# Order of PSUM banks and copies where the lag shrinks, and a new order of the last chunk, in a fused attention and mixture-of-adapters kernel

## The chip, the core and the metric

The kernel runs on one core of a Trainium2 chip. The metric is device time in microseconds for one launch, taken as the median of several runs. Each engine (PE for matrix products, DVE for vector work, ACT for activations, POOL, and SP, which issues most transfers) works through its own list of instructions in order and waits on semaphores of the others.

## What is computed

Attention over pooled keys, followed by a mixture of eight low-rank adapters with the two best kept per token:

```python
kv_pool = kv.reshape(B, H // r, r, W // r, r, C).mean(axis=(2, 4))
kv_flat = kv_pool.reshape(B, -1, C) @ w_sr            # keys and values
a = softmax(q @ k.T / sqrt(C));  x = a @ v
logits = x @ w_gate                                   # the 2 best of 8 experts
out = x + sum over the 2 experts of w_e * (x @ A[e]) @ B[e]
```

There are 4 batches of 12288 tokens with 128 features; each batch has 768 pooled keys. The result is 49152 x 128 in float32.

## The kernel before, in words

The tokens go in 96 chunks of 512 (`NCH` = 96), 24 to a batch. A software pipeline runs over the loop variable `c`. In each pass PE makes the scores of a later chunk (line 329, three pairs of products, each followed by an exponential on ACT, line 330), weighs the values of chunk c-1 in two halves (`weigh`, line 341), and turns x of chunk c-2 (`turned`, line 408: four products with the identity into the bank `tp`). After the second half of `weigh`, DVE normalises chunk c-1: a reciprocal (line 348), the multiplication into `xn_all` (line 352), and four MAX8 (line 359). The sums of `weigh` have one pair of banks (`ps_x`, one buffer), so the first product of the next pass waits until line 352 has read them.

The adapter part of chunk x is done later, by a lag that shrinks with x because the gates travel through DRAM and back:

- `gated_hidden(x)` (lines 440 to 449): one product of A with the turned x (line 443), and one DVE operation that multiplies by the gates and writes `ht` (line 446). It is done in pass x + lag(x).
- `up(x)` (line 489): four products of `ht` with B; then `give(x)`: DVE adds x (line 503) into `osb`, and every second time SP stores a pair of chunks (line 522).
- `evacuate` (line 419): DVE copies the turned x out of its bank into `xt`, of which there are seven buffers.

Both `gated_hidden` and `up` use the one bank of `mtile` (tag `hd`) unless they are given another; the turned x uses the one bank of `ps_t` (tag `tp`, also got by `t_bank()`). The lag is 9 for x below 57, 8 below 67, 7 below 81, then 6 (line 675). Where it falls by one, a pass gets two of something. From lines 677 to 679: passes 65, 74 and 87 have two `gated_hidden`, and passes 69, 78 and 91 have two `up`. In these six passes a second piece of work goes into the bank `tp` (line 708), which the turned x of the same pass needs a little later. In every pass the order of the DVE list is: adds of `up`, normalise, last `gated_hidden`, (in odd passes) the transpose of the gates, then the copy of line 419.

The last two chunks, n-1 = 94 and n = 95, are done behind the loop in an order written out by hand (lines 834 to 911), with banks of their own. There every chunk is stored by itself, 256 KB each: the chunks n-7 to n-1 by SP in the order n-7, n-5, n-6, n-3, n-2, n-1, n-4, and chunk n by ACT's queue (line 911). `take` (line 494) copies a finished bank to `osb` on ACT, `turn` (line 795) turns h by products with the identity and copies it out on ACT (line 801) or DVE (line 803), `x_first` (line 481) puts x into a bank by products with the identity so that B's product is added on top. `all_ok` (lines 578 to 584) counts range flags with two products and two small DVE operations, whose result `bad` every engine loads (line 915) to decide on a slow path that isn't taken here. The two DVE operations of `count_sum(1)` (lines 571 and 572) belong to the same check.

Of the kernel before, what the change touches and what calls it, by code (L numbers as in the profile page):

```python
# [21 lines left out]
def kernel(  # L22
# [11 lines left out]
    P = 128  # L34
    B, N, C = q.tensor.shape
# [5 lines left out]
    NTOK = 512  # L41
    NS = NTOK // P
# [3 lines left out]
    NCH = B * CPB  # L46
# [16 lines left out]
        name="ps_x", bufs=1, side="right", space=bass.MemoryType.PSUM))  # L63
# [5 lines left out]
    def mtile(shape, dtype=FP32, name="hd"):  # L69
        return ps_h.tile(shape, dtype, tag="hd", name=name)  # L70

    mm = nc.tensor.matmul
# [75 lines left out]
    id_f32 = const.tile([P, P], FP32)  # L148
# [111 lines left out]
    def squares(b, t):  # L260

        v = vext[b][:, 2 * t:2 * t + 2, 0:C + G]
        sq = keep.tile([P, 2, C + G], FP32, name=f"sq{b}") if t == 0 else small.tile(
            [P, 2, C + G], FP32, tag="sq", name="sq", bufs=1)
        nc.gpsimd.tensor_tensor(sq, v, v, op=ALU.mult)
        if t == 0:
            sqsum[b] = sq
        else:
            nc.gpsimd.tensor_tensor(sqsum[b], sqsum[b], sq, op=ALU.add)
# [45 lines left out]
    tt, xps, xpair, xn, gw, gin, xT, hg, hgT, hps = {}, {}, {}, {}, {}, {}, {}, {}, {}, {}  # L315
# [124 lines left out]
    def gated_hidden(c, bank=None):  # L440

        h_ps = mtile([P, NS, P], name="h_ps") if bank is None else as_tokens(bank)
        mm(h_ps, a_bf, xT[c], start=True, stop=True)  # L443
        hgT[c] = run.tile([P, NS, P], BF16, tag="ht", name="ht", bufs=4)
        h = c % 2 * NS // 2
        nc.vector.scalar_tensor_tensor(  # L446
            hgT[c].rearrange("p (k a) t -> p k (a t)", k=2),
            gE[c // 2][:, h:h + NS // 2].rearrange("p a t k -> p k (a t)"), 1.0,
            h_ps.rearrange("p (k a) t -> p k (a t)", k=2), op0=ALU.add, op1=ALU.mult)

    def as_tokens(bank):
        return bank.rearrange("p (s c) -> p s c", s=NS)
# [22 lines left out]
    dps = {}  # L475

    def x_first(c, bank, lo, hi):

        dps[c] = as_tokens(bank) if lo == 0 else dps[c]
        for s in range(lo, hi):  # L480
            mm(dps[c][:, s], id_f32, xn[c][:, s, 0:C], start=(s == 0), stop=False,
               skip_group_check=True)

    def up(c, bank=None):
        fresh = c not in dps
        if fresh:
            dps[c] = mtile([P, NS, P], name="d_ps") if bank is None else as_tokens(bank)
        for s in range(NS):
            mm(dps[c][:, s], columns(hgT[c], c, s), b_bf, start=(s == 0 and fresh),  # L489
               stop=(s == NS - 1), skip_group_check=True)  # L490

    def take(c, lo=0, hi=NS):
        osb = half_out()
        nc.scalar.activation(osb[:, lo:hi], dps[c][:, lo:hi], AF.Copy)
        return osb
# [10 lines left out]
    def put(c, osb, lo=0, hi=NS, queue=None):  # L506
        t0 = c // 2 * HROWS
        (queue or nc.sync).dma_start(
            out[t0:t0 + HROWS, :].rearrange("(p k s) c -> p k s c", p=P, k=2)[:, c % 2, lo:hi],
            osb[:, lo:hi])  # L510
# [28 lines left out]
    CUT = NCH - 15  # L539
# [38 lines left out]
    def all_ok(bank):  # L578
        n = (NCH - CUT) * NS
        mm(bank[0:1, 0:n], ones_c, ok[:, tail], start=True, stop=False)  # L580
        mm(bank[0:1, 0:n], ones_c, low, start=False, stop=True)
        nc.vector.tensor_reduce(last, bank[0:1, 0:n], axis=AX.X, op=ALU.add)
        full = float(P * (NCH * NS + n) + P * 2 * B + 2 * B)
        nc.vector.tensor_scalar(bad, last, tot, full, op0=ALU.add, op1=ALU.not_equal)
# [17 lines left out]
    def t_bank():  # L602
        return ps_t.tile([P, NTOK], FP32, tag="tp", name="t_ps")
# [72 lines left out]
    sent, fetched, made, ups = {}, {}, {}, {}  # L676
# [9 lines left out]
    for c in range(2, NCH - 1):  # L686
        b, k = divmod(c, CPB)
        if c in fetched and lag(2 * fetched[c] + 1) > 8:
            load_gates(fetched[c])
        if c % 2 == 0 and c // 2 + 3 < 2 * NQ:  # L690
            turn_q(c // 2 + 3)
        if c % 2 and (c + 11) // 2 < 2 * NQ:
            load_q((c + 11) // 2)
        if c == 2:
            load_q(6)
        next_scores()
        weigh(c - 1, 0)
        if c == NCH - 2:
            down(c - 4, stile("h_ps")[:, 0])
            apply_gate(c - 4)  # L700
        next_scores()
        if c in tanhs:
            gate_tanhs(tanhs[c])
        two = len(made.get(c, ())) > 1
        if two:
            gated_hidden(made[c][0])
        for x in ups.get(c, ()):
            up(x, t_bank() if two or x != ups[c][0] else None)
            give(x)
        if c in fetched and lag(2 * fetched[c] + 1) <= 8:  # L710
            load_gates(fetched[c])
        weigh(c - 1, 1)
        prep_step(c)
        if c == CUT + 5:
            count_sum(0)
        normalise(c - 1)
        if c % 2 == 0:
            gate(c // 2 - 1, nc.gpsimd)
            if c // 2 + 4 < 2 * NQ:
                cast_q(c // 2 + 4)  # L720
        _, evacuate = turned("x", c - 2)
        if c == NCH - 2:
            _, evacuate_h = turned("h", c - 4, stile("t_ps")[:, 0])
        next_scores()
        prep(c)
        k0 = 19
        if k in (k0, k0 + 2, k0 + 4) and b + 1 < B:
            if b == 0:
                squares(0, (k - k0) // 2)
            squares(b + 1, (k - k0) // 2)  # L730
        for x in made.get(c, ())[-1:]:
            gated_hidden(x)
        if c in sent:
            send_gates(sent[c])
        if c == NCH - 2:
            down(c - 3, stile("h_ps")[:, 0])
            apply_gate(c - 3)
        evacuate(c == NCH - 2)
        if c == NCH - 2:
            evacuate_h(True)  # L740

        if c in (32, 40, 56, 80):
            ranges((32, 40, 56, 80).index(c))
        a = slice(0, CUT * NS)
        if CUT < c <= CUT + 3:
            count_ok(a, c - CUT - 1, flags[:, 0:1])
        elif c == CUT + 4:
            values_ok()
        elif c == CUT + 5:
            count_sum(1)  # L750


# [4 lines left out]
        name="ps_e", bufs=1, reuse_waits="tile", space=bass.MemoryType.PSUM))  # L757

    def bank(i):
        return ps_e.tile([P, NTOK], FP32, tag=f"e{i}", name=f"e{i}")  # L760
# [30 lines left out]
    def turn(src, lo, hi, bank_, store, key, act=True):  # L791

        t_ps = bank_.bitcast(BF16)[:, 0:(hi - lo) * P].rearrange("p (s c) -> p s c", c=P)
        for s in range(lo, hi):
            mm(t_ps[:, s - lo], src[:, s], id_bf, is_transpose=True,
               start=(s == lo), stop=(s == hi - 1), skip_group_check=True)
        if key not in store:
            x_or_h = ("xt", 7) if store is xT else ("ht", 4)
            store[key] = run.tile([P, NS, P], BF16, tag=x_or_h[0], name="xr", bufs=x_or_h[1])
        if act:  # L800
            nc.scalar.activation(store[key][:, lo:hi], t_ps, AF.Copy)
        else:
            nc.vector.tensor_copy(store[key][:, lo:hi], t_ps)
# [10 lines left out]
    n = NCH - 1  # L814
# [8 lines left out]
    def tops4(c, top, y):  # L823
# [20 lines left out]
        name="ps_f", bufs=1, side="right", space=bass.MemoryType.PSUM))  # L844

    def fbank(i):
        return ps_f.tile([P, NTOK], FP32, tag=f"f{i}", name=f"f{i}")

    _, evacuate = turned("x", n - 2)
# [36 lines left out]
    x3 = ps_e.tile([P, 2, 512], FP32, tag="y5", name="x3")  # L886
# [2 lines left out]
    gate_w(0, NS, nc.gpsimd, arg5, msk5)  # L889
    gated(n, 0, NS, arg5, h5)  # L890
    x_first(n - 1, fbank(1), 2, 4)
    up(n - 1)
    o4 = take(n - 1)
    put(n - 1, o4)
    add(n - 4, o1, nc.gpsimd)
    put(n - 4, o1)
    d5 = as_tokens(x3[:, 1])
    for s in range(2):
        mm(d5[:, s], id_f32, xn[n][:, s, 0:C], start=(s == 0), stop=False, skip_group_check=True)
    turn(hg[n], 0, 2, bank(0), hgT, n)  # L900
    turn(hg[n], 2, 4, t_bank(), hgT, n, False)
    all_ok(bank(1))
    for s in range(2):
        mm(d5[:, s], hgT[n][:, s], b_bf, start=False, stop=(s == 1), skip_group_check=True)
    o5 = half_out()
    nc.scalar.activation(o5[:, 0:2], d5[:, 0:2], AF.Copy)
    d6 = as_tokens(mtile([P, NTOK], name="d6"))
    for s in range(2, 4):
        mm(d6[:, s - 2], hgT[n][:, s], b_bf, start=(s == 2), stop=(s == 3), skip_group_check=True)
    nc.vector.tensor_tensor(o5[:, 2:4], d6[:, 0:2], xn[n][:, 2:4, 0:C], op=ALU.add)  # L910
    put(n, o5, queue=nc.scalar)

    end_banks.close()
    ps_g = ctx.enter_context(tc.tile_pool(name="ps_g", bufs=1, space=bass.MemoryType.PSUM))
# [3 lines left out]
    with tc.If(bad_v != 0):  # L918
# [11 lines left out]
        with tc.For_i(0, B) as b:  # L930
            nc.sync.dma_start(kp, kp_all[bass.ds(b, 1)].rearrange("o p k -> p (o k)"))
            for h in range(2):
                s = slice(h * NKV // 2, (h + 1) * NKV // 2)
# [3 lines left out]
            for h in range(2):  # L937
                v_ps = mtile([P, NJ // 2, C + E], name="gv_ps")
                for g in range(NJ // 2):
                    j = h * NJ // 2 + g  # L940
                    mm(v_ps[:, g], kp[:, j * P:(j + 1) * P], wext,
                       start=(g == 0), stop=(g == NJ // 2 - 1))
# [96 lines left out]
```

## Time and profile before

| what | value |
|---|---|
| median of 3 runs | 373.58 us (373.55 to 374.5) |
| the profiled execution | 374.4 us, span 372.6 us from first to last instruction |
| mean granted clock of PE | 0.999 |
| busy: PE, ACT, DVE, POOL | 355.7, 308.3, 300.3, 223.7 us |
| idle before line 330 (ACT), until PE gave the scores | 37.7 us |
| idle before line 503 (DVE), until PE gave the products of `up` | 31.9 us |
| moved by DMA | 101.01 MB, mean 271 GB/s |

Busy times are sums over the span; PE's matrix products are pipelined and their ends are modelled, so the start of the next product tells more than an end. Times given as "250.24" are microseconds from the start of the span. Rows of a timeline read: start, length, engine, line, operation, out<-in, and in brackets the engine's idle time before it and what ended it. The span is 1.8 us shorter than the execution's own time.

### The profile page before, as it was taken

What the parts mean: (1) busy time and instruction counts of PE and PEld (TensorE: products, weight loads), DVE (VectorE), ACT (ScalarE), POOL (GpSimd) and SP (SyncE); (2) the same over time, 40 slices, a digit from 0 to 9 for tenths busy, and PEclk for the clock granted to TensorE, in tenths of its full rate; (3) what the DMA queues carried; (4) which work ended last, traced back from release to release, by engine and by line L of the source; (5) the groups of instructions that cost most, each with busy time, mean ns of one, the idle gap of its engine ahead of it and who ended that gap; (6) DMA issues with size and microseconds to landing.
All of it is one profiled execution on the core that took longest, in us unless ns stands there. A gap on an engine that the chain in (4) does not pass through costs nothing.

```text
span 372.6 us, 10601 instructions
## 1 busy us (share of the span) xinstructions
PE 355.7 (95%) x3945; PEld 264.3 (71%) x3945; DVE 300.3 (81%) x953; ACT 308.3 (83%) x390; POOL 223.7 (60%) x374
## 2 busy tenths in 40 slices
PE   4889999999999999999999999999999999999984
PEld 1456777777777777777777777777777767767773
DVE  3785558878888888888888888888788889988894
ACT  1579999889888888889889889898887978978843
POOL 1013799978599879693497879693454235223253
PEclk9999999999999999999999999999999999999999
DMA  7998999999999999999999999998678699754324
GB/s 264 419 354 218 318 289 311 302 298 276 288 375 294 316 305 303 285 298 294 305 316 305 349 341 285 319 274 266 207 213 277 195 244 231 215 132 130 144 114 173
DMA packets 83818, 101.01 MB, mean 271 GB/s; under 512 B 58804, under 2 KB 59060, under 8 KB 83764
## 3 DMA queue, kind: packets, MB, share of 16 engines
q1 hardware_dynamic: 83332, 99.98, 93.6%
q8 instruction: 31, 0.51, 0.6%
q10 hardware_dynamic: 432, 0.33, 0.3%
q14 instruction: 23, 0.19, 0.1%
HBM read 62.33 MB, written 25.90 MB: 237 GB/s over the span
## 4 chain that ended last, share of the span: by engine, by line
PE 87%; DVE 5%; ACT 3%; DMA 2%; issue 1%; POOL 1%; SPq 0%; ACTq 0%; DVEq 0%
PE xps L341 34%; PE sg L329 32%; PE t_ps L408 6%; PE h_ps L443 5%; PE d_ps L489 5%; DMA kvt<-in_kv_dram 2%; ACT tt L330 2%; DVE osb L503 1%; PE v_ps L218 1%; DVE ht L446 1%; DVE kvt L194 1%; PE k_ps L243 1%; PE w_ps L609 1%; PE kp_ps L210 0%; ACT qT L597 0%
## 5 line engine op out<-in xcount | busy, mean ns | idle before, releaser
L330 ACT ACTIVATE tt<-sg 128x1024 f16<-128x1024 f32 x288 | 276.3, 1023 | 38.0 <-PE sg L329 37.7
L329 PE MATMUL sg<-qT,kfT 128*128 128x512 f16 x576 | 170.2, 379 | 0.5 <-ACT qT L597 0.3
L341 PEld LDWEIGHTS <-tt 128*128 128x128 f16 x2304 | 146.6, 98 | 26.9 <-DVE xn_all L352 15.4
L341 PE MATMUL xps<-vext,tt 128*128 128x136 f16 x2256 | 164.6, 223 | 0.3 <-DVE xn_all L352 0.2
L503 DVE TENSOR_TENSOR osb<-d_ps,xn_all 128x512 f32<-128x512 f32 x82 | 56.7, 691 | 32.0 <-PE d_ps L489 31.9
L368 POOL TENSOR_TENSOR arg<-xn_all,top 128x64 f32<-128x64 f32 x47 | 14.4, 307 | 99.9 <-DVE top L359 93.4
L352 DVE TENSOR_TENSOR xn_all<-xps,rinv_all 128x540 f32<-128x540 f32 x94 | 67.7, 720 | 3.3
L329 PEld LDWEIGHTS <-kfT 128*128 128x128 f16 x576 | 49.1, 98 | 24.6 <-issue 1.8
L194 POOL TENSOR_TENSOR kvt<-kvt 128x1024 f32<-128x1024 f32 x27 | 63.7, 2361 | 2.0 <-PE xps L341 1.9
L446 DVE SCALAR_TENSOR_TENSOR ht<-ge,h_ps 128x512 bf16<-128x512 f16 x90 | 60.5, 672 | 1.3 <-PE h_ps L443 0.9
L108 POOL CAST q<-q 128x1024 f16<-128x1024 f32 x45 | 46.8, 1041 | 24.1 <-DMA q<-in_q_dram 24.1
L489 PEld LDWEIGHTS <-ht 128*128 128x128 bf16 x368 | 27.7, 98 | 21.3 <-issue 1.3
L359 DVE MAX8 top<-xn_all 128x8 f32<-128x8 f32 x376 | 35.1, 156 | 6.3
L408 PE MATMUL t_ps<-id_bf,xn_all 128*128 128x128 bf16 x376 | 36.3, 219 | 2.5 <-DVE osb L503 2.5
L419 DVE COPY xt<-t_ps 128x512 bf16<-128x512 bf16 x92 | 36.8, 400 | 0.0
L443 PE MATMUL h_ps<-xt,a_bf 128*128 128x512 bf16 x90 | 34.1, 379 | 0.1
L489 PE MATMUL d_ps<-b_bf,ht 128*128 128x128 bf16 x328 | 31.7, 219 | 0.0
L408 PEld LDWEIGHTS <-xn_all 128*128 128x128 bf16 x376 | 26.1, 98 | 3.6 <-issue 3.3
L348 DVE RECIPROCAL rinv_all<-xps 128x4 f32<-128x4 f32 x94 | 17.1, 182 | 12.9 <-PE xps L341 11.5
L371 POOL TENSOR_SCALAR msk<-msk 128x64 f32<-128x64 f32 x47 | 20.1, 428 | 4.1
L372 POOL TENSOR_TENSOR arg<-arg,msk 128x64 f32<-128x64 f32 x47 | 15.0, 320 | 3.9
L370 POOL TENSOR_TENSOR arg<-arg,msk 128x64 f32<-128x64 f32 x47 | 15.0, 319 | 3.7
(150 smaller groups left out, 221.0 us busy)
## 6 DMA issues: line engine op xcount, KB each, us to landing
kvt<-in_kv_dram SPq DMA_DIRECT2D x48, 512.0 KB
q<-in_q_dram SPq DMA_DIRECT2D x46, 512.0 KB
out_dram<-osb SPq DMA_DIRECT2D x44, 512.0 KB
ge<-g_h SPq DMA_DIRECT2D x45, 256.0 KB
out_dram<-osb SPq DMA_DIRECT2D x7, 256.0 KB
q<-in_q_dram SPq DMA_DIRECT2D x1, 1024.0 KB
qT<-q SPq DMA_TRANSPOSE x46
g_h<-g_sb SPq DMA_DIRECT2D x45, 16.0 KB
```

Of the source, the lines that this page charges most:

```text
L108: nc.gpsimd.tensor_copy(q16[i], q32[i].rearrange("p k n -> p (k n)"))
L194: eng.tensor_tensor(v[:, 0], v[:, 0], v[:, d], op=ALU.add)
L329: mm(sg[:, k], kfT[b][:, j * P:(j + 1) * P], qc, start=True, stop=True)
L330: nc.scalar.activation(tt[c][:, 2 * r:2 * r + 2], sg, AF.Exp, bias=0.0, scale=scale)
L341: mm(o, tt[c][:, j, s * P:(s + 1) * P], vext[b][:, j, 0:VW], start=(j == 0 and s % 2 == 0), stop=(j == NJ - 1 and s % 2 == 1), skip_group_ ...
L352: nc.vector.tensor_tensor(xn[c][:, :, 0:C + G].rearrange("p (b s) v -> p b s v", b=2), xv[:, :, :, 0:C + G], ri.rearrange("p (b s) -> p b ...
L408: mm(columns(t_ps, c, s), src[:, s], id_bf, is_transpose=True, start=(s == 0), stop=(s == NS - 1), skip_group_check=True)
L419: nc.vector.tensor_copy(to, t_ps)
L443: mm(h_ps, a_bf, xT[c], start=True, stop=True)
L446: nc.vector.scalar_tensor_tensor(hgT[c].rearrange("p (k a) t -> p k (a t)", k=2), gE[c // 2][:, h:h + NS // 2].rearrange("p a t k -> p k ( ...
L489: mm(dps[c][:, s], columns(hgT[c], c, s), b_bf, start=(s == 0 and fresh), stop=(s == NS - 1), skip_group_check=True)
L503: nc.vector.tensor_tensor(osb[:, lo:hi], d, xn[c][:, lo:hi, 0:C], op=ALU.add)
```

## The change

There are two parts. In the six passes, the extra piece of work in bank `tp` is now the first of the pass and the last piece takes `hd`: in passes 65, 74 and 87 the first `gated_hidden` goes to `tp` and `up` to `hd`; in passes 69, 78 and 91 the first `up` goes to `tp` and the second to `hd`. In the pass ahead of each (64, 68, 73, 77, 86, 90) the copy of line 419 is put on DVE's list before the last `gated_hidden` instead of behind it. `count_sum(1)` moves from pass 86 to pass 88.

In the tail, the products that put the first half of x of chunk n into its bank now come ahead of `up(n-1)` (and in another bank); the products that turn the last h come directly behind `up(n-1)`; `take(n-1)` and the stores of n-1 and n-4 follow behind the turn, so on ACT the copy of the turned h stands ahead of `take(n-1)`. The two DVE operations of the range check stand behind the last store.

```diff
+    def flag(bank):
+        n = (NCH - CUT) * NS
         nc.vector.tensor_reduce(last, bank[0:1, 0:n], axis=AX.X, op=ALU.add)
...
-        two = len(made.get(c, ())) > 1
-        if two:
-            gated_hidden(made[c][0])
+        for x in made.get(c, ())[:-1]:
+            gated_hidden(x, t_bank())
         for x in ups.get(c, ()):
-            up(x, t_bank() if two or x != ups[c][0] else None)
+            up(x, None if x == ups[c][-1] else t_bank())
             give(x)
...
+        early = max(len(made.get(c + 1, ())), len(ups.get(c + 1, ()))) > 1
+        if early:
+            evacuate()
         for x in made.get(c, ())[-1:]:
             gated_hidden(x)
...
-        evacuate(c == NCH - 2)
+        if not early:
+            evacuate(c == NCH - 2)
...
-        elif c == CUT + 5:
+        elif c == CUT + 7:
             count_sum(1)
...
     x_first(n - 1, fbank(1), 2, 4)
+    d5 = bank(0)
+    x_first(n, d5, 0, 2)
     up(n - 1)
+    turn(hg[n], 0, 2, x3[:, 1], hgT, n)
+    turn(hg[n], 2, 4, t_bank(), hgT, n, False)
     o4 = take(n - 1)
     put(n - 1, o4)
     add(n - 4, o1, nc.gpsimd)
     put(n - 4, o1)
-    d5 = as_tokens(x3[:, 1])
-    for s in range(2):
-        mm(d5[:, s], id_f32, xn[n][:, s, 0:C], start=(s == 0), stop=False, skip_group_check=True)
-    turn(hg[n], 0, 2, bank(0), hgT, n)
-    turn(hg[n], 2, 4, t_bank(), hgT, n, False)
-    all_ok(bank(1))
+    count = mtile([P, NTOK], name="count")
+    all_ok(count)
+    d5 = dps[n]
     for s in range(2):
         mm(d5[:, s], hgT[n][:, s], b_bf, start=False, stop=(s == 1), skip_group_check=True)
...
-    d6 = as_tokens(mtile([P, NTOK], name="d6"))
+    d6 = as_tokens(bank(1))
...
     put(n, o5, queue=nc.scalar)
+    flag(count)
```

## The prediction, made before the changed kernel ran

> **What bounds the kernel now.** I read the page first, then the waits of PE, then the timeline around the passes that the change touches, then the end.
>
> ```profile
> span 372.6 us, 10601 instructions
> PE 87%; DVE 5%; ACT 3%; DMA 2%; issue 1%; POOL 1%; SPq 0%; ACTq 0%; DVEq 0%
> ```
>
> The chain that ended last runs through PE for 87% of the span. In the loop a gap on PE is therefore lost time, unless another engine would have stopped PE a little later anyway. PE's list of waits has one entry that fits the change:
>
> ```profile
> PE t_ps L408 <- DVE osb L503: 2.5, 6, 0.4
> ```
>
> Six times the turning of x (line 408) waits until DVE's add (line 503) has read the bank `tp`. These are the six passes with a second piece of work in that bank. Pass 64, an ordinary one, and pass 65 stand side by side in the timeline:
>
> ```profile
> 246.65 0.87 PE L341 MATMUL xps<-vext,tt 128*128 128x136 f16 x12
> 247.36 0.39 PE L408 MATMUL t_ps<-id_bf,xn_all 128*128 128x128 bf16 x4
> 247.78 0.72 DVE L352 TENSOR_TENSOR xn_all<-xps,rinv_all 128x540 f32<-128x540 f32 x1
> 248.02 0.38 PE L443 MATMUL h_ps<-xt,a_bf 128*128 128x512 bf16 x1
> 248.53 0.37 DVE L359 MAX8 top<-xn_all 128x8 f32<-128x8 f32 x4
> 248.66 0.87 PE L341 MATMUL xps<-vext,tt 128*128 128x136 f16 x12
> 248.82 0.67 DVE L446 SCALAR_TENSOR_TENSOR ht<-ge,h_ps 128x512 bf16<-128x512 f16 x1
> 249.41 0.42 DVE L419 COPY xt<-t_ps 128x512 bf16<-128x512 bf16 x1
> 249.81 0.38 PE L443 MATMUL h_ps<-xt,a_bf 128*128 128x512 bf16 x1
> 250.02 0.39 PE L489 MATMUL t_ps<-b_bf,ht 128*128 128x128 bf16 x4
> 250.22 0.69 DVE L446 SCALAR_TENSOR_TENSOR ht<-ge,h_ps 128x512 bf16<-128x512 f16 x1 [0.39 <-PE h_ps L443]
> 250.24 0.87 PE L341 MATMUL xps<-vext,tt 128*128 128x136 f16 x12
> 250.83 0.68 DVE L503 TENSOR_TENSOR osb<-t_ps,xn_all 128x512 f32<-128x512 f32 x1
> 251.43 0.17 DVE L348 RECIPROCAL rinv_all<-xps 128x4 f32<-128x4 f32 x1
> 251.56 0.38 PE L408 MATMUL t_ps<-id_bf,xn_all 128*128 128x128 bf16 x4 [0.45 <-DVE osb L503]
> 251.63 0.72 DVE L352 TENSOR_TENSOR xn_all<-xps,rinv_all 128x540 f32<-128x540 f32 x1
> 252.86 0.34 PE L341 MATMUL xps<-vext,tt 128*128 128x136 f16 x3
> ```
>
> In pass 64 the turn starts 247.36 - 246.65 = 0.71 after `weigh`'s second half; in pass 65 it starts 251.56 - 250.24 = 1.32 after. So 0.61 is lost, more than the row's 0.45, as that counts from a modelled end. From the turn to the next pass's first L341 both passes take 1.30.
>
> A pass with two `up` has the same pattern (pass 78):
>
> ```profile
> 297.40 0.87 PE L341 MATMUL xps<-vext,tt 128*128 128x136 f16 x12
> 298.71 0.38 PE L408 MATMUL t_ps<-id_bf,xn_all 128*128 128x128 bf16 x4 [0.44 <-DVE osb L503]
> 298.78 0.72 DVE L352 TENSOR_TENSOR xn_all<-xps,rinv_all 128x540 f32<-128x540 f32 x1
> 300.01 0.87 PE L341 MATMUL xps<-vext,tt 128*128 128x136 f16 x12
> ```
>
> **The six passes, step by step.** No instruction is added or removed; two change places.
>
> *The stall goes.* In pass 65 bank `tp` is now filled by the first product (249.81) and emptied by the first DVE operation instead of the second. That one ends at 250.22 + 0.69 = 250.91. DVE's end at 251.51 let PE start at 251.56, so a release costs 0.05: the bank is free at 250.96. The turn would come by itself at 250.24 + 0.71 = 250.95. In pass 78 it is the first add that empties the bank, one operation earlier than now, with the same distance. The 0.61 is gone.
>
> *What is late next.* The DVE list still holds one more operation of about 0.6 than an ordinary pass, so the reciprocal stays where it is, at 251.43, and line 352 still ends at 251.63 + 0.72 = 252.35. The next pass's first L341 needs the banks that line 352 reads. In pass 64 it started 248.66 - 248.50 = 0.16 behind that end; PE would have been there at the same moment by itself (247.36 + 1.30). With the stall gone PE arrives at 250.95 + 1.30 = 252.25, before line 352 has ended, and **a new wait** takes the place of part of the old one: start at 252.35 + 0.16 = 252.51 instead of 252.86, a gain of 0.35. Behind this product on PE stands the whole next pass. In pass 78 it is 300.01 - (299.50 + 0.16) = 0.35 too. The 0.16 is an upper end of what the release costs; the lowest seen is the 0.05 above, which would make the gain 0.46. I take 0.35, the row of the same two operations. Whether the whole gap of 0.51 is needed no row excludes, so the lower end is nothing.
>
> *The copy ahead of the product with the gates.* In pass 64 the copy takes the place at 248.82, its bank having been full since 247.75; operations follow each other on DVE up to 0.08 before the reported end (248.82 + 0.67 against 249.41), so `ht` starts near 249.16 and ends near 249.85 instead of 249.49. Who waits for `ht`: `up` in bank `hd`, at 250.02. With the release that is 249.90, 0.12 early; if the copy takes its full 0.42, 0.05 early. In the passes where it is late by up to 0.1, that is hidden too, since the reciprocal then has 0.3 to spare before it moves. The first product of pass 65 waits for the copy instead of `ht`; it gets earlier. There is one added wait: seven `xt` buffers and a lag of 9 mean that in pass 64 the copy overwrites the slot which line 443 of the same pass still reads. That product ran from 248.02 to 248.40, ahead of 248.82, so the copy finds it done; were it later, DVE would stand with `ht` and the next normalise behind it.
>
> *The check's two small operations*, moved from pass 86 to 88, I cost at nothing:
>
> ```profile
> 328.82 0.69 DVE L446 SCALAR_TENSOR_TENSOR ht<-ge,h_ps 128x512 bf16<-128x512 f16 x1 [0.23 <-PE h_ps L443]
> ```
>
> With them in front, DVE still stood idle for 0.23. Without that cover the price is at most their own half microsecond in one pass.
>
> Sum of the loop: 6 x 0.35 = **2.1 less**, between 0 and 6 x 0.46 = 2.8.
>
> **The tail.** The rows of the last two chunks:
>
> ```profile
> 365.38 0.60 ACT L801 ACTIVATE xr<-e 128x512 bf16<-128x512 bf16 x1 [0.59 <-PE e L795]
> 366.03 0.40 PE L489 MATMUL f<-b_bf,xr 128*128 128x128 bf16 x4 [0.25 <-ACT xr L801]
> 366.28 0.71 PE L899 MATMUL x<-xn_all,id_f 128*128 128x128 f32 x4
> 366.47 0.60 ACT L494 ACTIVATE osb<-f 128x512 f32<-128x512 f32 x1 [0.49 <-PE f L489]
> 366.83 0.28 PE L795 MATMUL e<-id_bf,hgs 128*128 128x128 bf16 x2
> 367.20 0.38 ACT L801 ACTIVATE xr<-e 128x256 bf16<-128x256 bf16 x1
> 367.96 0.38 ACT L906 ACTIVATE osb<-x 128x256 f32<-128x256 f32 x1 [0.38 <-PE x L904]
> 368.07 0.42 DVE L910 TENSOR_TENSOR osb<-d,xn_all 128x256 f32<-128x256 f32 x1
> ```
>
> The pair with x of chunk n holds PE for 366.83 - 366.28 = 0.55. Now it goes into the gap before `up(n-1)`, and that starts about 0.14 late, near 366.17. The turn of the last h follows 0.25 later, at 366.42 instead of 366.83: **0.41 earlier**. All that hangs on it moves by this: ACT's copy to 366.79, the last add to an end near 368.08, so the store of chunk n goes out 0.41 earlier. But on ACT `take(n-1)` now stands behind that copy: from 366.47 it moves to about 367.05, so the stores of n-1 and, behind it on SP, n-4 go out **0.58 later**.
>
> ```profile
> 367.09 0.92 SPq L508 DMA_DIRECT2D out_dram<-osb  x2
> 368.57 0.36 ACTq L508 DMA_DIRECT2D out_dram<-osb  x1
> 367.00:368.00 1.00, 0.88 (x12) 0.45 (x9) 0.64 (x3) 0.49 (x3) 0.00 (x0) 1.00 0.22 76
> 368.00:369.00 1.00, 0.03 (x1) 0.00 (x0) 0.42 (x1) 0.34 (x1) 0.00 (x0) 1.00 1.00 381
> 369.00:370.00 1.00, 0.00 (x0) 0.00 (x0) 0.00 (x0) 0.00 (x0) 0.00 (x0) 1.00 0.85 326
> 370.00:371.00 1.00, 0.00 (x0) 0.00 (x0) 0.00 (x0) 0.00 (x0) 0.00 (x0) 1.00 0.26 98
> ```
>
> The last two columns of the stretches are the DMA share and GB/s. Three stores of 262 KB take 786 KB / 381 GB/s = 2.06 at full rate. They run from about 367.8 (0.22 of the first stretch) to about 370.2, with little idle between them. After the change the first starts at about 368.4 and the other two are already issued when it ends: 368.4 + 2.1 = 370.5. The end is **0.4 later** although the last store leaves 0.41 earlier. The ends: 0.41 less, if chunk n's store alone sets the end, and 0.6 more, if all of the delay shows.
>
> The Trainium skill ("DMA: Bandwidth & Descriptors", section Issuing engines are not separate DMA queues) says that transfers started by different engines run on the same 16 DMA engines and interleave, so a second issuing engine saves only the issue. It speaks against this half of the change; by it the tail gives the 0.4 more, without it the 0.41 less. The DMA share of 1.00 agrees with it.
>
> The range check's two DVE operations now end some 0.4 later than before; every engine loads `bad` and then waits for the stores, which land later still, so nothing; without that cover, 0.4.
>
> **Sum.** -2.1 + 0.4 = -1.7 on the profiled 374.4 (span 372.6, so 370.9). The median of the runs, 373.58, lies 0.8 below the profiled execution; the difference is taken from it: **371.9**.
>
> **Rivals.**
>
> *The end follows the last store alone* (0.12): -2.1 - 0.41 gives 371.1. For it: that store was issued 1.5 after the first. Against: the stretches leave no idle DMA to take it.
>
> *The new wait is shorter* (0.10): 0.05 behind line 352 instead of 0.16; -2.8 + 0.4 gives 371.2. Against: the weights of that product have to be loaded first.
>
> *Half the places gain* (0.15): the later `ht` holds `up`, and the next pass's DVE list does not catch up, in one kind of pass; -1.05 + 0.4 gives 372.9.
>
> *Everything in the loop is given back* (0.15): the next pass's L341 needs the whole 0.51 behind line 352, because DVE, with its extra operation, is the real clock of these passes. Then the tail alone is left: +0.4 to +0.6, 374.1. It decides if that L341 stays where it is when the turn comes earlier. Against: the ordinary pass manages with 0.16. A third of this (0.05) is the case in which the earlier copy also holds `ht` and delays `up` by some 0.12 in each of the six: 374.1 + 0.7 = 374.8.
>
> **How the numbers follow.** My forecast has the rest, 0.48. The range 370.9 to 373.3 leaves out only the last rival and some spread. About 0.3%, 1.1 us, is what a measurement here can tell from no change. Faster by more (below 372.5): 0.48 + 0.12 + 0.10 = 0.70. Within: 0.15 + 0.10 = 0.25. Slower by more (above 374.7): 0.05.
>
> **What would show it.** PE's wait of line 408 for line 503 gone, and in its place six short idle times of PE before line 341 that line 352 ends; the next pass's L341 0.51 behind line 352 would prove the giving back. In the tail: `take(n-1)` behind the copy of the turned h on ACT, the last add 0.4 nearer to the loop's end, and the DMA at full share until later than before, counted from `up(n-1)`. The prediction is wrong if PE waits for `ht` or the copy in the six passes, or if the DMA stands idle between the last stores.

## The result and the profile after

| | before | after |
|---|---|---|
| median of 6 runs, same chip | 373.73 us (373.55 to 374.5) | 371.57 us (371.27 to 371.88) |
| profiled execution, span | 374.4, 372.6 | 371.88, 370.1 |
| first to last turn of x in the loop (line 408) | 326.0 | 323.4 |
| second `x_first(n-1)` to the span's end | 7.50 | 7.42 |

After to before is 0.9938 [0.9925, 0.9950]: 1.9 to 2.8 us less. The changed kernel is on a later line count from line 582 on; its line 803 is line 795 of before, 809 and 811 are 801 and 803, 915 and 919 are 906 and 910.

The last two rows of the table split the time. The loop's length is read from the row of all products of line 408, asked for by line; its last two times are the first and the last start. Before, and then after:

```profile
L408 PE MATMUL t_ps<-id_bf,xn_all x376: 216/219/231, 32.6 to 358.6; 128*128 128x128 bf16 x188
```

```profile
L408 PE MATMUL t_ps<-id_bf,xn_all x376: 216/220/231, 32.8 to 356.2; 128*128 128x128 bf16 x188
```

Between them lies a loop that is 2.6 shorter. For the tail I count from a fixed place, the second set of products of line 481 (`x_first(n-1, ..., 2, 4)`), called **the mark** from here on: 365.12 before, 362.68 after.

```profile
365.12 0.44 PE L481 MATMUL f<-xn_all,id_f 128*128 128x128 f32 x2
```

(The row is cut by the window's end; its start counts.) The span ends 7.50 behind the mark before and 7.42 after. So the 2.5 of the profiles came from the loop (2.66 by the starts of its turns, less 0.22 by which the loop began later, and 0.08 more from the tail), and the tail gave next to nothing either way.

The page's first line, and the chain that ended last, after:

```profile
span 370.1 us, 10598 instructions
PE 89%; DVE 3%; ACT 3%; DMA 2%; issue 1%; POOL 1%; SPq 0%; ACTq 0%; DVEq 0%
```

DVE's part of the chain fell from 5% to 3%: line 503 has 0.6 us of it, where it had 4.6. The list of waits has no row of line 408 any more. Passes 64 and 65 in the timeline after:

```profile
248.75 0.37 DVE L359 MAX8 top<-xn_all 128x8 f32<-128x8 f32 x4
249.04 0.40 DVE L419 COPY xt<-t_ps 128x512 bf16<-128x512 bf16 x1
249.36 0.68 DVE L446 SCALAR_TENSOR_TENSOR ht<-ge,h_ps 128x512 bf16<-128x512 f16 x1
250.02 0.38 PE L443 MATMUL t_ps<-xt,a_bf 128*128 128x512 bf16 x1
250.24 0.39 PE L489 MATMUL d_ps<-b_bf,ht 128*128 128x128 bf16 x4
250.44 0.69 DVE L446 SCALAR_TENSOR_TENSOR ht<-ge,t_ps 128x512 bf16<-128x512 f16 x1 [0.40 <-PE t_ps L443]
250.46 0.87 PE L341 MATMUL xps<-vext,tt 128*128 128x136 f16 x12
251.04 0.68 DVE L503 TENSOR_TENSOR osb<-d_ps,xn_all 128x512 f32<-128x512 f32 x1
251.18 0.38 PE L408 MATMUL t_ps<-id_bf,xn_all 128*128 128x128 bf16 x4
251.64 0.17 DVE L348 RECIPROCAL rinv_all<-xps 128x4 f32<-128x4 f32 x1
251.85 0.72 DVE L352 TENSOR_TENSOR xn_all<-xps,rinv_all 128x540 f32<-128x540 f32 x1
252.63 0.59 PE L341 MATMUL xps<-vext,tt 128*128 128x136 f16 x7
```

The turn starts 251.18 - 250.46 = 0.72 behind the second half of `weigh` (1.32 before): the stall is gone. Line 352 ends at 251.85 + 0.72 = 252.57, which is 2.11 behind that half, the same as before: DVE's list did not move. The next pass's L341 starts at 252.63, **0.06** behind that end and 1.45 behind the turn (1.30 before). So there is a new wait, of 0.15. From the second half of `weigh` to the next pass's first L341 it is 2.17 instead of 2.62, a gain of 0.45. Pass 78 has the same picture:

```profile
296.27 0.87 PE L341 MATMUL xps<-vext,tt 128*128 128x136 f16 x12
296.99 0.38 PE L408 MATMUL t_ps<-id_bf,xn_all 128*128 128x128 bf16 x4
297.66 0.72 DVE L352 TENSOR_TENSOR xn_all<-xps,rinv_all 128x540 f32<-128x540 f32 x1
298.43 0.65 PEld L341 LDWEIGHTS <-tt 128*128 128x128 f16 x11 [0.48 <-DVE xn_all L352]
```

The new wait stands in brackets at the weight load (PEld), not at the product. In the list of waits, too, it appears only there; PE's own row for L341 has not grown, as the ends of the products are modelled and lie behind the true ones. First the row of before, then of after, with total, times and longest:

```profile
PEld L341 <- DVE xn_all L352: 15.4, 61, 0.7
```

```profile
PEld L341 <- DVE xn_all L352: 17.8, 66, 0.7
```

The tail after, from the mark to the last operation, and the four stretches of 1 us behind it (the last two columns are the DMA share and GB/s):

```profile
362.68 0.66 PE L481 MATMUL f<-xn_all,id_f 128*128 128x128 f32 x4
363.18 0.61 PE L481 MATMUL e<-xn_all,id_f 128*128 128x128 f32 x4
363.62 0.39 PE L489 MATMUL f<-b_bf,xr 128*128 128x128 bf16 x4
363.85 0.28 PE L803 MATMUL x<-id_bf,hgs 128*128 128x128 bf16 x2
364.21 0.38 ACT L809 ACTIVATE xr<-x 128x256 bf16<-128x256 bf16 x1 [0.68 <-PE x L803]
364.49 0.59 ACT L494 ACTIVATE osb<-f 128x512 f32<-128x512 f32 x1
365.08 0.43 DVE L919 TENSOR_TENSOR osb<-e,xn_all 128x256 f32<-128x256 f32 x1 [0.45 <-PE e L918]
365.59 0.36 ACTq L508 DMA_DIRECT2D out_dram<-osb  x1
365.66 0.20 DVE L587 TENSOR_SCALAR bad<-last,tot 1x1 int32<-1x1 f32 x1
```

```profile
365.00:366.00 1.00, 0.05 (x1) 0.00 (x0) 0.74 (x3) 0.36 (x2) 0.00 (x0) 1.00 0.04 16
366.00:367.00 1.00, 0.00 (x0) 0.00 (x0) 0.00 (x0) 0.00 (x0) 0.00 (x0) 1.00 1.01 379
367.00:368.00 1.00, 0.00 (x0) 0.00 (x0) 0.00 (x0) 0.00 (x0) 0.00 (x0) 0.77 1.00 377
368.00:369.00 1.00, 0.00 (x0) 0.00 (x0) 0.00 (x0) 0.00 (x0) 0.00 (x0) 0.50 0.17 47
```

`up(n-1)` starts 0.94 behind the mark (0.91 before), the last add ends 2.83 behind it (3.38 before), the last store leaves at 2.91 (3.45), and the stores of n-1 and n-4 at 2.43 and 2.86 (1.97 and 2.40). Then the DMA is full for two microseconds with nothing else running.

### The profile page after: what moved, and what is told of

Its sections match the earlier page's. It is cut to its first block, busy times and chain, and to the rows that moved or that the text cites. A ratio compares the mean times of both kernels' runs of the same rounds, so it can differ in the third digit from the quotient of the medians.

```text
span 370.1 us, 10598 instructions
## 1 busy us (share of the span) xinstructions
PE 355.1 (96%) x3944; PEld 263.6 (71%) x3945; DVE 299.9 (81%) x953; ACT 308.7 (83%) x390; POOL 223.8 (60%) x374
## 4 chain that ended last, share of the span: by engine, by line
PE 89%; DVE 3%; ACT 3%; DMA 2%; issue 1%; POOL 1%; SPq 0%; ACTq 0%; DVEq 0%
PE xps L341 36%; PE sg L329 33%; PE t_ps L408 6%; PE d_ps L489 5%; PE h_ps L443 5%; DMA kvt<-in_kv_dram 2%; ACT tt L330 2%; PE v_ps L218 1%; DVE kvt L194 1%; PE k_ps L243 1%; PE w_ps L612 1%; PE kp_ps L210 0%; ACT qT L600 0%; DVE xn_all L352 0%; PE y L341 0%
## 5 line engine op out<-in xcount | busy, mean ns | idle before, releaser
L341 PEld LDWEIGHTS <-tt 128*128 128x128 f16 x2304 | 146.2, 98 | 28.2 <-DVE xn_all L352 17.8
L341 PE MATMUL xps<-vext,tt 128*128 128x136 f16 x2256 | 164.7, 223 | 0.3 <-DVE xn_all L352 0.2
L503 DVE TENSOR_TENSOR osb<-d_ps,xn_all 128x512 f32<-128x512 f32 x85 | 58.7, 691 | 27.7 <-PE d_ps L489 27.1
L446 DVE SCALAR_TENSOR_TENSOR ht<-ge,h_ps 128x512 bf16<-128x512 f16 x87 | 58.5, 672 | 0.4
L489 PE MATMUL d_ps<-b_bf,ht 128*128 128x128 bf16 x340 | 32.9, 220 | 0.0
L443 PE MATMUL h_ps<-xt,a_bf 128*128 128x512 bf16 x86 | 32.6, 379 | 0.1
```

What stands on the lines that cost most here:

```text
L341: mm(o, tt[c][:, j, s * P:(s + 1) * P], vext[b][:, j, 0:VW], start=(j == 0 and s % 2 == 0), stop=(j == NJ - 1 and s % 2 == 1), skip_group_ ...
L446: nc.vector.scalar_tensor_tensor(hgT[c].rearrange("p (k a) t -> p k (a t)", k=2), gE[c // 2][:, h:h + NS // 2].rearrange("p a t k -> p k ( ...
L503: nc.vector.tensor_tensor(osb[:, lo:hi], d, xn[c][:, lo:hi, 0:C], op=ALU.add)
```

## The experiments

All ratios are to the kernel before, run on the same chip, with a 95% interval. Runs e1 to e4 shared one set of runs of before (median 373.73), e5 to e8 another on that chip (374.25), e9 to e12 a third, on another chip (374.29). Single profiles of these kernels differ by some tenths in the start-up: the turn of pass 8 comes at 50.13 to 51.55 among them, while passes 8 to 60, which no edit touches, take 182.17 to 182.18 in each. The medians, too, differ by more between two sets of runs than their intervals say: `e10_loop_again` below is the same kernel as `e1_loop`, and has 0.9919 [0.9904, 0.9934] where e1 has 0.9950 [0.9936, 0.9963]. That is why the loop is judged by its length and by each pass, and why a few tenths between medians decide nothing here.

**Each part alone.** `e1_loop` takes the loop's part of the diff and keeps the tail of before; `e2_tail` is the reverse; `e3_banks` takes from the loop's part the banks only:

```diff
-        two = len(made.get(c, ())) > 1
-        if two:
-            gated_hidden(made[c][0])
+        for x in made.get(c, ())[:-1]:
+            gated_hidden(x, t_bank())
         for x in ups.get(c, ()):
-            up(x, t_bank() if two or x != ups[c][0] else None)
+            up(x, None if x == ups[c][-1] else t_bank())
```

and `e4_early` the early copy (with `count_sum` in pass 88) only:

```diff
+        early = max(len(made.get(c + 1, ())), len(ups.get(c + 1, ()))) > 1
+        if early:
+            evacuate()
         for x in made.get(c, ())[-1:]:
             gated_hidden(x)
...
-        evacuate(c == NCH - 2)
+        if not early:
+            evacuate(c == NCH - 2)
```

*e1_loop.* Expected:

> The six passes, the early copies and the move of the two check operations as in the change; the tail as before. My theory from the traces: each of the six passes gives back 0.44 (the turn at its own time, then the next pass's L341 only 0.06 behind line 352), so 6 x 0.44 = 2.6 less than before, a ratio near 0.993. The forecast's step (0.16 behind line 352) would be 2.1 less, 0.9944. If the tail brought half of the result, this one would be only 1.1 less, 0.997.

Measured: 371.73, 0.9950 [0.9936, 0.9963].

```profile
L408 PE MATMUL t_ps<-id_bf,xn_all x376: 216/219/233, 31.9 to 355.3; 128*128 128x128 bf16 x188
```

The loop has the length of the changed kernel's, 323.4. Pass by pass its turns have moved by the same amounts: 0.60 ahead in pass 65, 0.16 back in pass 66, and so in five of the six. In pass 69 PE has two more products (line 226) ahead of the turn, and it is 0.50 ahead and 0.04 back. That is 2.66 in all. The median is 2.0 below before, less than the 2.6 that was expected; the trace shows 0.44 in five passes and 0.46 in pass 69. The loop's part alone makes the result.

*e2_tail.* Expected:

> The tail as in the change; the loop as before. My theory: compute is 0.4 nearer to its end, but the stores of chunks n-1 and n-4 leave 0.5 later and the three last stores then share the DMA; between 0 and 0.5 slower than before, ratio 1.000 to 1.0013. Rival: the last store alone sets the end, 0.4 less, ratio 0.999.

Measured: 374.18, 1.0009 [0.9998, 1.0020]; every pass of the loop within 0.01 of before, and the span's end 7.39 behind the mark. The expected 0 to 0.5 more lies inside the interval, and so does nothing at all; 0.4 less, the rival, does not. Its profile shows no cost.

*e3_banks.* Expected:

> Only the banks exchanged, no early copy and no move of the check operations; the tail as before. My theory: the stall of line 408 goes, but in passes 65, 74, 78 and 91 the first product into bank tp waits for the late copy, by 0.07, 0.23, 0.23 and 0.07 as the rows of before give it, so 0.6 of the 2.6 is lost: about 2.0 less than before, ratio 0.9946. Rival: the early copy carries the change, and the banks alone bring nothing: ratio 1.000.

Measured: 372.18, 0.9966 [0.9953, 0.9979]. The median fell by 1.55, less than expected, but the turns are 2.06 earlier than before, as expected, so the early copy is worth 0.60 beside the banks. Passes 65, 74, 78 and 91 lose 0.07, 0.23, 0.23 and 0.08, as expected to within 0.01. Without the early copy, the first product of pass 74 waits for the copy, here the last operation of its list:

```profile
281.18 0.38 DVE L419 COPY xt<-t_ps 128x512 bf16<-128x512 bf16 x1
...
281.62 0.38 PE L443 MATMUL t_ps<-xt,a_bf 128*128 128x512 bf16 x1
```

The product starts 0.06 behind the copy's end. This is the part that the diff does not show: once the first piece of the pass decides when bank `tp` is free, the copy that feeds it is on the path.

*e4_early.* Expected:

> Only the early copies and the move of the check operations; banks and tail as before. My theory: line 408 still waits for the add of line 503 (0.4 to 0.45, six times) and the time is as before within 0.1. Rival: the early copy carries the change: 2 less, ratio 0.9945.

Measured: 374.84, 1.0033 [1.0020, 1.0046]: a miss. All six stalls of line 408 are still there, as they must be, but the loop is 0.41 longer (passes 65, 74, 78 and 91 lose 0.08, 0.13, 0.13 and 0.06). Around the start of pass 74:

```profile
282.24 0.41 DVE L419 COPY xt<-t_ps 128x512 bf16<-128x512 bf16 x1
282.56 0.68 DVE L446 SCALAR_TENSOR_TENSOR ht<-ge,h_ps 128x512 bf16<-128x512 f16 x1
...
283.29 0.38 PE L443 MATMUL h_ps<-xt,a_bf 128*128 128x512 bf16 x1
```

With the old banks the first product of pass 74 goes into `hd`, which `ht` of pass 73 still reads; `ht` ends at 283.24 and the product starts 0.05 later. The early copy has pushed `ht`, and `ht` is what this product waits for. The two edits of the loop thus need each other: with the new banks the product waits for the copy and gains by the order, with the old ones it waits for `ht` and loses. The rest of the 1.1 is not in the passes, and its cause stays open: in the profile pass 8 starts 0.46 later than in before (51.45 against 50.99), but the tail is 0.37 shorter.

**What holds the next pass now.** `e7_spread` takes one DVE operation out of the six passes: the add of the last `up` is done by ACT (copy) and POOL (add):

```diff
+        if spread:
+            nc.scalar.activation(o[:, c % 2], dps[c], AF.Copy)
+            nc.gpsimd.tensor_tensor(o[:, c % 2], o[:, c % 2], xn[c][:, :, 0:C], op=ALU.add)
+        else:
+            add_rows(c, osb=o[:, c % 2])
...
-            give(x)
+            give(x, x == ups[c][-1] and max(len(made.get(c, ())), len(ups[c])) > 1)
```

> The changed kernel, but in the six passes the add of the last up is taken off DVE: ACT copies the bank and POOL adds x. My theory: the 0.15 that is left of the stall in each pass comes from DVE's extra operation ahead of line 352; without it the next pass's L341 starts 1.30 behind the turn again, 6 x 0.15 = 0.9 less than the changed kernel, ratio 0.9915 to the kernel before. Rival: ACT, with 0.6 more in these passes, gives its last exponential late, and the products of the next pass wait for it: no gain or up to 6 x 0.3 lost.

Measured: 371.67, 0.9927 [0.9914, 0.9940], the loop as long as after (323.4). Neither expectation holds as stated. In the two even passes, 74 and 78, the new wait is gone and 0.15 gained. Pass 78:

```profile
297.14 0.38 PE L408 MATMUL t_ps<-id_bf,xn_all 128*128 128x128 bf16 x4
...
298.44 0.34 PE L341 MATMUL xps<-vext,tt 128*128 128x136 f16 x3
```

298.44 - 297.14 = 1.30, the distance of an ordinary pass. In the four odd passes 0.09, 0.13, 0.06 and 0.05 are lost: there ACT first has the gates' tanh to do (line 384), it empties bank `hd` later, and the product of line 443 behind it waits. Pass 65:

```profile
251.30 0.32 ACT L384 ACTIVATE gw_all<-arg 128x64 f16<-128x64 f32 x1
251.54 0.60 ACT L520 ACTIVATE osb<-d_ps 128x512 f32<-128x512 f32 x1
...
252.19 0.38 PE L443 MATMUL h_ps<-xt,a_bf 128*128 128x512 bf16 x1
```

So the 0.15 that is left in a pass is DVE's list of operations, as passes 74 and 78 show, but this way of shortening it gives it back in the odd ones.

**The tail's order.** Four edits of the changed kernel. `e5_swap` issues the store of n-4 ahead of n-1:

```diff
-    o4 = take(n - 1)
-    put(n - 1, o4)
     add(n - 4, o1, nc.gpsimd)
     put(n - 4, o1)
+    o4 = take(n - 1)
+    put(n - 1, o4)
```

> The changed kernel, but SP stores chunk n-4 ahead of chunk n-1 (its add on POOL ends 0.8 before the copy of n-1). My theory: the end of the changed kernel is set by three stores that share the DMA; in its profile the DMA stands idle for about a microsecond before them. With n-4 sent into that gap, the end comes 0.5 to 0.7 earlier than in the changed kernel: 2.7 to 3.0 below the kernel before, ratio 0.992 to 0.9928. Rival: the last store alone sets the end, so nothing changes: ratio as the changed kernel, 0.994.

Measured: 370.83, 0.9906 [0.9892, 0.9919]; stores at 1.64, 2.43 and 2.91 behind the mark, the span's end at 6.69 instead of 7.42, 0.73 earlier: about as expected, in a single profile.

`e6_take_first` keeps the order of the stores and puts `take(n-1)` back ahead of the copy of the turned h:

```diff
-    turn(hg[n], 0, 2, x3[:, 1], hgT, n)
-    turn(hg[n], 2, 4, t_bank(), hgT, n, False)
     o4 = take(n - 1)
     put(n - 1, o4)
+    turn(hg[n], 0, 2, x3[:, 1], hgT, n)
+    turn(hg[n], 2, 4, t_bank(), hgT, n, False)
```

> The changed kernel, but the copy of n-1 on ACT and its store stand ahead of the turn of the last h, as before the change. My theory: the stores of n-1 and n-4 leave 0.45 earlier, the copy of the turned h and so the last store 0.3 later; the three stores no longer queue, and the end is up to 0.2 earlier than in the changed kernel or equal. Rival (the last store alone sets the end): 0.3 later.

Measured: 370.68, 0.9903 [0.9889, 0.9918]; stores at 1.99, 2.43 and 3.23, the last one 0.32 later than after, and yet the end at 6.50, 0.9 earlier, where at most 0.2 was expected; the rival is out. In a stretch of its tail the DMA is full as it was after:

```profile
366.00:367.00 1.00, 0.00 (x0) 0.00 (x0) 0.00 (x0) 0.00 (x0) 0.00 (x0) 1.00 0.99 377
```

`e8_pair_behind` moves the pair with x of chunk n from ahead of `up(n-1)` to behind the turn:

```diff
-    x_first(n, d5, 0, 2)
     up(n - 1)
     turn(hg[n], 0, 2, x3[:, 1], hgT, n)
     turn(hg[n], 2, 4, t_bank(), hgT, n, False)
+    x_first(n, d5, 0, 2)
```

> The changed kernel, but the pair of products that puts x of chunk n into its bank comes behind the turn of the last h instead of ahead of up(n-1). The forecast has the pair delay up(n-1) by 0.14; then the last add ends 0.1 earlier and the end 0.1 earlier, too little to tell by the times, but to be read from the start of up(n-1). Rival: the pair then delays the last products of B, and the last add ends up to 0.5 later.

Measured: 370.96, 0.9910 [0.9896, 0.9924], the profiled execution at 372.14, its end at 7.25. The pair's place:

```profile
363.02 0.66 PE L481 MATMUL f<-xn_all,id_f 128*128 128x128 f32 x4
363.93 0.40 PE L489 MATMUL f<-b_bf,xr 128*128 128x128 bf16 x4 [0.25 <-ACT xr L809]
...
365.75 0.42 DVE L919 TENSOR_TENSOR osb<-e,xn_all 128x256 f32<-128x256 f32 x1 [0.77 <-PE e L918]
```

`up(n-1)` is at 0.91 behind the mark: the pair ahead of it costs 0.03, since it fits almost whole into a gap in which PE waits for ACT's copy. Behind the turn the same pair delays the last add by 0.32 (end at 3.15), so the rival held.

`e11_both` joins e5 and e6:

```diff
-    turn(hg[n], 0, 2, x3[:, 1], hgT, n)
-    turn(hg[n], 2, 4, t_bank(), hgT, n, False)
-    o4 = take(n - 1)
-    put(n - 1, o4)
     add(n - 4, o1, nc.gpsimd)
     put(n - 4, o1)
+    o4 = take(n - 1)
+    put(n - 1, o4)
+    turn(hg[n], 0, 2, x3[:, 1], hgT, n)
+    turn(hg[n], 2, 4, t_bank(), hgT, n, False)
```

> The changed kernel with both repairs of the tail: SP stores n-4 ahead of n-1, and the copy of n-1 on ACT stands ahead of the turn. All stores but the last leave early; the last one 0.3 later than in the changed kernel. If the three stores sharing the DMA set the end of the changed kernel, this is 0.5 to 0.9 below it; if the last store alone did, 0.3 above it.

Measured: 371.37, 0.9916 [0.9902, 0.9931]: a miss. The stores leave at 1.63, 2.07 and 3.23, and the end is at 7.39, not ahead of either.

**The tail by itself.** On the third set, the changed kernel once more (`e9_after_again`), `e1_loop` once more (`e10_loop_again`), and `e12_no_store`, the changed kernel without the store of chunk n-4 (512 rows of the output are left out):

```diff
     add(n - 4, o1, nc.gpsimd)
-    put(n - 4, o1)
```

> The changed kernel once more, beside the next three on one chip. About 2.2 below the kernel before, ratio 0.9925 to 0.995.

> The loop part alone once more, beside the changed kernel. If the new tail costs 0.2 to 0.4, as the stores leave later, this one is that much below the changed kernel; if the new tail gains (last store 0.5 earlier), it is 0.4 above it.

> The changed kernel without the store of chunk n-4 (512 rows of the output are left out). If the three last stores share the DMA, one store less brings its transfer time, 0.5 to 0.7 below the changed kernel. If the last store alone sets the end, nothing changes.

Measured: e9 371.12, 0.9916 [0.9902, 0.9929], 3.2 below before, where 2.2 was expected; e10 371.30, 0.9919 [0.9904, 0.9934]; e12 370.63, 0.9902 [0.9887, 0.9917]. Old and new tail stand 0.2 apart with intervals that lie over each other, so neither side of e10's expectation is shown. With one store less the profile ends 6.30 behind the mark instead of 7.09 (e9); the median falls by 0.5, though the intervals overlap.

None of the variants beats the changed kernel for certain: the best, e6 with [0.9889, 0.9918], overlaps e9 with [0.9902, 0.9929].

## Why the prediction was nearly right, step by step

- *The stall of line 408 goes*, 0.61 in each pass: right. It is 0.60 in five passes and 0.50 in pass 69, in e1 as in the changed kernel.
- *What is late next*: the mechanism was right and the size was not. The step "start at 252.35 + 0.16 = 252.51 instead of 252.86, a gain of 0.35" took for the release of the banks what pass 64 showed between line 352's end and L341. There PE came at that moment by itself, as the prediction says; the distance was no wait. In the six passes, where PE does wait, it is 0.05 to 0.06, the same as the 0.05 from line 503 to line 408. The gain is 0.44 in five passes and 0.46 in pass 69, 2.66 in all, not 2.1. The rival "The new wait is shorter" had this number and 0.10 of the chance.
- *The copy ahead of the product with the gates*: hidden, as forecast, in the changed kernel. The copy takes the place of 0.32 on DVE (249.04 to 249.36), `ht` ends at 250.04, and `up` needs it at 250.24. What the forecast did not price is what its absence costs: 0.60 (e3). The early copy alone, without the banks, costs 0.41 (e4).
- *`count_sum` in pass 88* at nothing: right, no step at pass 86 or 88 beyond those of pass 87.
- *The tail*: "near 366.17", a delay of `up(n-1)` by 0.14, was 0.03 (e8 moves the pair away and gets 0.03 back). The last add is 0.55 earlier against the mark, not 0.41, and the stores of n-1 and n-4 are 0.46 later, not 0.58. The last store thus leaves 0.54 earlier and three stores still end up on one DMA, at full share.
- The step "The end is **0.4 later**" failed. Its own numbers, 370.5 against 370.2, give 0.3. Measured in the profiles it is 0.1 earlier, and over five profiles with the old tail and four with the new the end lies 7.18 and 7.22 behind the mark on average; the medians (e2 against before, e9 against e10) are too wide to decide. That the three stores share the DMA is right: e12, with one less, ends earlier, and e5, with an earlier first store, too. Here the Trainium skill ("DMA: Bandwidth & Descriptors", section Issuing engines are not separate DMA queues) agrees with the traces: after, from 4.27 to 5.07 behind the mark, the packets of SP's queue have 48% of the 16 engines and those of ACT's 52%. What failed is that the end of before was not set by the shared rate; see the last section.
- *The sum*: -2.66 and about nothing, where -2.1 + 0.4 was forecast. The two errors, 0.56 and 0.4, are of the same sign, so by the working the time should have missed by about 1. The profiles moved by 2.5, and the medians by 2.2 (e9's set: 3.2). That 371.57 came within 0.3 of 371.9 is therefore luck: this set's medians moved by less than the loop did, within the spread from set to set that e1 and e10 show.

The 0.03 for the pair and the place of the stores are shown by e5, e6 and e8. Only argued is why the end did not follow them: it is read from the traces and was not tried by itself.

## What to carry to other kernels

When a wait is taken away, the floor under it is priced from a place where the same wait truly stops the engine, not from a place where the engine happened to arrive later: 0.06 against 0.16 here, 0.6 us over six passes. Two edits that change banks and an order are one edit if each decides what the other's operation waits for; alone, one gave 2.06 and the other cost 0.41, and together they gave 2.66. At the end of a kernel, look at the last landing of each DMA engine before taking the issue time of a store for its end.

## What the runs showed of the hardware that was not expected

Transfers of instructions fall into the last stores. The DMA view of before, over the stretch 366.7 to 368.2, lists them among the queues (packets, MB, share of 16 engines):

```profile
q1 hardware_dynamic: 137, 0.25, 45.4%
q8 instruction: 1, 0.02, 3.6%
```

The second row is one packet of 16 KB, which occupies one of the 16 engines for 0.88 us (3.6% of 16 x 1.5); in other profiles up to 1.7 us. From 1.7 to 1.9 behind the mark, while it is under way, the packets of the stores keep 14.9 engines busy. (Queue q14 has further instruction packets, of 8 KB, near the end; they took 0.3 to 0.6 us.) The share of the stores that lies on this engine comes late. In before, 15 of 16 engines have delivered their part of the last store 5.60 behind the mark, and the last one at 6.53. In the stretch from 5.18 to 6.18 the DMA is 0.10 busy, that is 1.6 engines of 16, one with what is left of the stores and the rest with two of q14's packets:

```profile
370.30:371.30 1.00, 0.00 (x0) 0.00 (x0) 0.00 (x0) 0.00 (x0) 0.00 (x0) 1.00 0.10 39
```

In the five profiles with the old tail (before, e1, e3, e4, e10) such a packet starts 0.47 to 1.64 behind the mark, the fifteenth engine lands its part of the last store at 5.51 to 5.99 (mean 5.67) and the last one at 5.93 to 6.53 (mean 6.21): the engine that has fallen behind has no pause long enough to make it up before the next store, and stays behind to the end. The span ends 0.97 to 1.03 behind that last landing in all nine profiles named here.

In the four with the new tail (after, e2, e7, e9) the fifteenth lands at 5.89 to 6.10 (mean 6.02), 0.35 later, near the forecast 0.4, but the last at 5.95 to 6.39 (mean 6.19). In e9 the packet starts at 0.42 and makes the last landing of the store of n-2 late (3.66, the fifteenth at 2.75), but the store of n-1 starts so late now that it lands evenly (4.46 and 4.51); in after, e2 and e7 the packet starts only at 5.50 to 5.65. So the delay is there in 15 engines of 16, and what decides the end is the sixteenth, which was as late before.

In e11 the packet took 1.28 from 2.38 behind the mark, amid the stores, and the last landing came at 6.42, 1.14 behind the fifteenth; the fifteenth, at 5.28, is 0.74 ahead of the new tail's mean, as much as its expectation asked for. In e6, whose end was the earliest of the four orders of the tail, the packet started at 5.37, when the last store had landed. That this explains e11's miss and the tail's nothing is a reading of the traces: no run moved the instruction transfer alone, and when it comes differs from profile to profile.

The Trainium skill ("Runtime: NRT & Kernel Launch", section Instruction fetch mechanics) says that instructions are refilled in blocks of 16 KiB by the sequencer's own DMA queue, at a cost that is mostly hidden. The size agrees with q8's packets of 16 KB; q14's are of 8 KB. By the reading above the cost is not hidden at this kernel's end, where 0.25 to 0.93 us lie between the fifteenth engine and the last in the old tail, and up to 1.14 in e11.

The release of PE by another engine costs little, and much the same in the five places where it was read: 0.05 from line 503 to line 408 before, 0.06 from line 352 to L341 after, 0.06 from the copy to line 443 in e3, 0.05 from `ht` to line 443 in e4, and 0.05 from ACT's copy to line 443 in e7.
